# The last output tiles of a recurrent scan with a gated unit: all down products first, two adds on GpSimd

## The chip, the cores and the metric

The kernel runs on one core of a Trainium2 chip. Its metric is the device time in microseconds (us) of one execution; lower is better. Five engines work side by side, each with its own queue of instructions: TensorE (PE, matrix products; PEld are its weight loads), VectorE (DVE), ScalarE (ACT), GpSimd (POOL), and SyncE (SP), which here only starts transfers. A number with the letter L is a line of the kernel's file.

## The reference

Input `x` has 2048 tokens of width 448, in bf16. It is normalised over its width, and two branches are computed from the result: a diagonal complex recurrence over the tokens (448 states) and a gated unit of width 1792.

```python
xn = _layernorm(x)
# branch A: h[t] = Lam_bar * h[t-1] + B_bar @ xn[t];  s = 2 * Re(C @ h) + xn * Dskip
s = _A_ref(xn, ...)
# branch B: h = sigmoid(xn @ w_gate) * (xn @ w_up);  _B_ref = h @ w_down
g = _silu(_B_ref(xn, w_gate, w_up, w_down))
return x + s * g
```

## The kernel before

The 2048 tokens are worked on in four chunks of 512 (`NCH`), each made of four tiles of 128 tokens (`TPC`). For every chunk the kernel multiplies by `w_gate` and `w_up` in 14 blocks of 128 columns (`FT`), multiplies by B, runs the scan on VectorE, multiplies the gated result by `w_down` (the "down" products, in `d_ps`), and multiplies the scanned states `h` by C (the "y" products, in `y_ps`). In the first three chunks these pieces are laid between each other by a written plan (`emit_line`, `group`, `fill`). The last chunk's down and y products come after that plan, in the plain code at the end of the function, and this is the part that the change touches.

The order of the instructions on each engine is the order in which the Python code issues them: `keep_order` (L60) ties every instruction to the one issued before it on the same engine. An engine therefore waits at the first instruction of its queue that isn't ready, whatever stands behind it.

The end of the last chunk (`c` is 3) is built from four helpers:

- `emit_down(j, ft0, ft1)` (L1110) issues the down products of output tile `j` for the blocks `ft0` to `ft1`, each a matmul of 128x128 weights with 448 columns. After the last block ScalarE takes Silu of the sum (L1115); the result `gs[c][:, j, :]`, called `g_t` in the profile, is the gate.
- `emit_rest_of(c, j)` (L841) computes on VectorE what doesn't depend on the y products: `t_g` = gated skip term (L843), and `t_x` = `t_g` + `x` (L848), kept in float32. The result is entered in `rests`.
- `emit_y(c, j, d0, d1)` (L850) issues the y products of tile `j`, seven matmuls for the columns `d0` to `d1`. If `j` isn't in `rests`, one more matmul with the identity adds the skip term to the sum.
- `emit_fin(c, j, d0, d1)` (L857) finishes a tile: `sg` = `y_ps` times the gate (L860, VectorE, read from PSUM), `o_l` = `sg` plus `t_x`, or plus `x` if there is no rest (L866, VectorE), and the store of `o_l` (L867, SyncE's queue).

Before the change, the end runs in this order: the down products of the tiles 0, 1 and 2 with their rests; ten of the fourteen down products of tile 3 (`late` is `FT - 4`); for the tiles 0, 1, 2 the y products, the multiplication, the add and the store; then the last four down products of tile 3; then the y products of tile 3 in two halves of 224 columns, each with its own identity matmul, multiplication, add and store. Tile 3 has no rest: its adds read `x`, in bf16.

Buffers rotate within a tag. `sg` lies in the tag `sigd` with four buffers; `t_g` and `o_l` share the tag `zb`, also with four. A fifth tile of a tag waits until the first one has been read.

Of the kernel before, what the change touches and what calls it, by code (L numbers as in the profile page):

```python
# [13 lines left out]
ALU = mybir.AluOpType  # L14
# [3 lines left out]
D = 448  # L18
F = 1792
P = 128  # L20
# [5 lines left out]
FT = F // P  # L26
# [25 lines left out]
def two_runs(ap: bass.AP, step: int, n: int) -> bass.AP:  # L52
    return bass.AP(tensor=ap.tensor, offset=ap.offset, ap=[*ap.ap[:-1], [step, 2], [1, n]])
# [18 lines left out]
def kernel(  # L72
# [18 lines left out]
    pe, act, dve, pool, sync = nc.tensor, nc.scalar, nc.vector, nc.gpsimd, nc.sync  # L91
# [8 lines left out]
    out_flat = out.rearrange("b s d -> (b s) d")  # L100
# [176 lines left out]
    def xn_runs(c, j):  # L277
        return two_runs(xn[c % 3][:, j, :], HD if c == 0 else DP - HD, HD)
# [562 lines left out]
    def emit_rest_of(c, j):  # L841
        t = op_.tile([P, D], BF16, name="t_g", tag="zb", bufs=4)
        dve.tensor_tensor(out=two_runs(t[:], HD, HD), in0=xn_runs(c, j), in1=two_runs(gs[c][:, j, :], HD, HD),  # L843
                          op=ALU.mult)
        if j % 2 == 0:
            room_of_rests.append(w.tile([P, 2, D], FP32, name="t_x", tag=("raw_re", "raw_c")[j // 2]))
        rests[j] = room_of_rests[j // 2][:, j % 2, :]
        dve.tensor_tensor(out=rests[j], in0=t[:], in1=x_t[c][:, j, :], op=ALU.add)  # L848

    def emit_y(c, j, d0=0, d1=D):  # L850
        ops = y_ops(c, j, slice(0, P), d0, d1, j not in rests)
        ys[c, j] = bank("y_ps", D)
        sm = Sum(ys[c, j], len(ops))
        for a in ops:
            sm.add(None, *a)

    def emit_fin(c, j, d0=0, d1=D):  # L857
        tt = c * TPC + j
        sg = op_.tile([P, D], BF16, name="sg", tag="sigd", bufs=4)
        dve.tensor_tensor(out=sg[:, d0:d1], in0=ys[c, j][:, d0:d1], in1=gs[c][:, j, d0:d1], op=ALU.mult)  # L860
        if j == 3:
            o = sp.tile([P, D], BF16, name="o_l", tag="ctmp")
        else:
            o = op_.tile([P, D], BF16, name="o_l", tag="zb", bufs=4)
        also = rests[j] if j in rests else x_t[c][:, j, :]
        dve.tensor_tensor(out=o[:, d0:d1], in0=sg[:, d0:d1], in1=also[:, d0:d1], op=ALU.add)  # L866
        sync.dma_start(out=out_flat[tt * P:(tt + 1) * P, d0:d1], in_=o[:, d0:d1])  # L867

# [232 lines left out]
    c = NCH - 1  # L1103
# [6 lines left out]
    def emit_down(j, ft0, ft1):  # L1110
        for ft in range(ft0, ft1):
            pe.matmul(ds[j][:], lhsT=hF[c, ft][:, j * P:(j + 1) * P], rhs=wd[:, ft, :], start=ft == 0,  # L1112
                      stop=ft == FT - 1)
        if ft1 == FT:
            act.activation(gs[c][:, j, :], ds[j][:], ACT.Silu)  # L1115

    late = FT - 4
# [8 lines left out]
    flush()  # L1126
    emit_down(2, 0, FT)
    emit_rest_of(c, 2)
    emit_down(3, 0, late)
    for j in range(3):  # L1130
        emit_y(c, j)
        emit_fin(c, j)
    emit_down(3, late, FT)

    for d0, d1 in ((0, D // 2), (D // 2, D)):
        emit_y(c, 3, d0, d1)
        emit_fin(c, 3, d0, d1)
# [31 lines left out]
```

## Time and profile before

| | |
|---|---|
| time, median of three runs (lowest, highest) | 182.96 us (182.48, 183.02) |
| the profiled execution: its time, its span | 182.26 us, 180.5 us |
| PE busy | 176.2 us (98% of the span) |
| DVE busy | 163.4 us (91%) |
| ACT busy | 115.1 us (64%) |
| POOL busy | 23.1 us (13%) |
| last POOL instruction | starts at 82.40 us |
| last instruction of DVE | starts at 177.79 us, lasts 0.27 us |

The span is the time from the first to the last event that the profiler saw; the time of an execution is longer by what lies around it, here 1.76 us. The shares are means over the whole span. PE is busy nearly always, but at the very end (after 177.3 us) it has nothing left to do, and the last instructions belong to DVE and to the store behind it. The trace also gives a granted clock for PE, which was at full speed (0.998).

### The profile page before, as it was taken

To read this page: it belongs to the slowest core of one execution; us is meant where nothing else is said; L and a number is where in the kernel's file an instruction comes from. 1 tells how busy PE (TensorE), PEld (TensorE's weight loads), DVE (VectorE), ACT (ScalarE), POOL (GpSimd) and SP (SyncE) were. 2 spreads that over 40 slices of the span, in tenths; PEclk is the share of its full clock that TensorE was granted. 3 is DMA by queue.
4 is the path that set the end of the run, shared out by engine and by line. 5 is a ranking of instruction groups with operands and counts; after the bars stand their busy time and mean duration, and the time that the engine had idled before them with its cause. 6 is when DMAs were issued, how large, how long until landed. Compare 5 with 4: busy or idle time off the path is not lost.

```text
span 180.5 us, 4326 instructions
## 1 busy us (share of the span) xinstructions
PE 176.2 (98%) x1637; PEld 88.2 (49%) x1637; DVE 163.4 (91%) x332; ACT 115.1 (64%) x240; POOL 23.1 (13%) x54
## 2 busy tenths in 40 slices
PE   7999999999999999999999999999999999999992
PEld 7764444445544444544544444544554444545552
DVE  4889999899999879999999999599999999499993
ACT  4999878979577887988177667047137577144100
POOL 3525668522000000003000000000000000000000
PEclk9999999999999999999999999999999999999999
DMA  5899998983442005021710020030010100011012
GB/s 150 239 292 211 245 176 168 356 185 77 99 83 53 16 4 131 5 69 36 89 31 0 4 56 2 4 102 0 4 29 0 35 0 2 4 53 51 0 32 73
DMA packets 26348, 14.27 MB, mean 79 GB/s; under 512 B 16083, under 2 KB 26070, under 8 KB 26326
## 3 DMA queue, kind: packets, MB, share of 16 engines
q1 hardware_dynamic: 26320, 13.98, 33.7%
q8 instruction: 13, 0.21, 0.5%
q14 instruction: 9, 0.07, 0.2%
q10 hardware_dynamic: 6, 0.00, 0.0%
HBM read 7.69 MB, written 1.84 MB: 53 GB/s over the span
## 4 chain that ended last, share of the span: by engine, by line
PE 97%; DVE 1%; issue 0%; DVEq 0%
PE g_ps L514 25%; PE u_ps L514 19%; PE d_ps L514 18%; PE bu L514 12%; PE y_ps L514 11%; PE d_ps L1112 6%; PE warm_ps L200 2%; PE g_ps L713 2%; PE u_ps L713 1%; PE tp_x L286 1%; DVE sg L860 0%; PE g_ps L706 0%; DVE o_l L866 0%; PE u_ps L706 0%; DVE xnT L289 0%
## 5 line engine op out<-in xcount | busy, mean ns | idle before, releaser
L514 PE MATMUL u_ps<-xnT,wu 64*128 64x512 bf16 x312 | 61.4, 376 | 0.0
L514 PE MATMUL g_ps<-xnT,wg 64*128 64x512 bf16 x312 | 53.4, 376 | 0.0
L752 ACT ACTIVATE sig<-g_ps 128x512 bf16<-128x512 f32 x52 | 29.2, 597 | 28.6 <-PE g_ps L514 28.0
L514 PE MATMUL bu<-xnT,bT 64*128 64x512 bf16 x168 | 37.4, 376 | 0.0
L514 PE MATMUL d_ps<-wd,hF 64*128 64x448 bf16 x336 | 32.3, 349 | 0.0
L514 PEld LDWEIGHTS <-wu 64*128 64x128 bf16 x312 | 22.4, 94 | 18.5
L752 ACT CAST ub<-u_ps 128x512 bf16<-128x512 f32 x52 | 29.3, 606 | 0.9 <-DVE hF L723 0.8
L514 PEld LDWEIGHTS <-wg 64*128 64x128 bf16 x312 | 18.9, 94 | 18.3 <-issue 0.4
L514 PEld LDWEIGHTS <-hF 64*128 64x128 bf16 x336 | 16.4, 94 | 15.6
L611 DVE TENSOR_TENSOR_SCAN wv<-r_col,st,ta 128x512 bf16<-128x512 f32 x18 | 22.7, 1277 | 0.2
L514 PE MATMUL y_ps<-ct,h 64*128 64x448 bf16 (+2 forms) x203 | 22.1, 343 | 0.0
L749 DVE TENSOR_TENSOR hF<-sig,ub 128x512 bf16<-128x512 bf16 x52 | 21.0, 413 | 0.4 <-ACT ub L752 0.3
L514 PEld LDWEIGHTS <-bT 64*128 64x128 bf16 x168 | 15.8, 94 | 10.0
L514 PE MATMUL g_ps<-xnT,wt 64*128 64x512 bf16 x52 | 19.6, 376 | 0.0
L514 PE MATMUL u_ps<-xnT,wt 64*128 64x512 bf16 x52 | 19.6, 376 | 0.0
L514 PEld LDWEIGHTS <-h 64*128 64x128 bf16 (+1 forms) x203 | 11.6, 95 | 9.9
L776 ACT ACTIVATE sigd<-d_ps 128x448 bf16<-128x448 f32 x12 | 6.6, 553 | 15.0 <-PE d_ps L514 15.0
L592 ACT CAST bus<-bu 128x512 bf16<-128x512 f32 x24 | 14.3, 597 | 1.7 <-PE bu L514 1.6
L514 PEld LDWEIGHTS <-wt 64*128 64x128 bf16 x104 | 9.8, 94 | 6.2
L831 DVE TENSOR_TENSOR o_t<-y_ps,xn 128x448 bf16<-128x448 f32 x12 | 6.9, 617 | 4.8 <-PE y_ps L514 4.8
L1112 PE MATMUL d_ps<-wd,hF 128*128 128x448 bf16 x56 | 10.9, 353 | 0.0
L244 POOL TENSOR_TENSOR rsd<-ve,mhalf 128x2 f32<-128x2 f32 (+2 forms) x5 | 4.6, 922 | 44.2 <-PE bu L514 44.1
(153 smaller groups left out, 239.7 us busy)
## 6 DMA issues: line engine op xcount, KB each, us to landing
wd<-in_B_w_down_dram SPq DMA_DIRECT2D x1, 1568.0 KB, 7.3
x<-in_A_x_dram SPq DMA_DIRECT2D x3, 448.0 KB, 5.0
out_dram<-o_t SPq DMA_DIRECT2D x6, 224.0 KB, 2.1
wg<-in_B_w_gate_dram SPq DMA_DIRECT2D x2, 256.0 KB, 3.6
wu<-in_B_w_up_dram SPq DMA_DIRECT2D x2, 256.0 KB, 3.7
bsw<-bus SPq DMA_DIRECT2D x4, 128.0 KB, 2.8
wsw<-wv SPq DMA_DIRECT2D x8, 64.0 KB, 1.9
c_re<-in_A_C_re_dram SPq DMA_DIRECT2D x1, 392.0 KB
```

The source lines that it names most:

```text
L200: pe.matmul(warm_ps[:], lhsT=t[:, 0:P], rhs=t[:, 0:P], start=True, stop=True)
L244: pool.tensor_tensor(out=rsd[:, t:t + n, :], in0=ve[:, t:t + n, :], in1=mhalf[:, 0:n, :], op=ALU.pow)
L286: pe.transpose(tps[j % 2][:, kt, :], xb[:, j, K_ROWS[kt]:K_ROWS[kt] + P], ident[:])
L514: m = pe.matmul(self.t[:, n0:n1], lhsT=lhsT, rhs=rhs, start=self.done == 1, stop=self.done == self.n)
L592: empty = [lambda cc=cc: act.copy(out=bus[:, cc, :], in_=pst[cc][:]) for cc in range(2)]
L611: dve.tensor_tensor_scan(out=T["wv"][:, cc, :], data0=rb, data1=T["ta"][:, cc, :], initial=(0.0 if c == 0 else st[pt][:, cc, :]), op0=mul, ...
L713: pe.matmul(t[:, n0:n1], lhsT=wm[:, k, f0:f1], rhs=xnT[c][:, kts[k], n0:n1], start=(first and k == 0), stop=(not first and last and k == 2))
L749: dve.tensor_tensor(out=h[:], in0=sig[:], in1=ub[:], op=ALU.mult)
L752: u.empty = [lambda: act.activation(sig[:], gt[:], ACT.Sigmoid), lambda: act.copy(out=ub[:], in_=ut[:])]
L776: act.activation(sigd[:], ds[j][:], ACT.Sigmoid)
L831: dve.tensor_tensor(out=two_runs(o[:, i, :], HD, HD), in0=two_runs(ys[c, j + 2 * i][:], HD, HD), in1=xn_runs(c, j + 2 * i), op=ALU.add)
L1112: pe.matmul(ds[j][:], lhsT=hF[c, ft][:, j * P:(j + 1) * P], rhs=wd[:, ft, :], start=ft == 0, stop=ft == FT - 1)
```

## The change

All fourteen down products of tile 3 now come before the first y product, and tile 3 gets a rest like the other three. With that, its y products have no identity matmul, and its two adds read the float32 `t_x` in place of the bf16 `x`. The add L866 of the tiles 0 and 2 is issued on GpSimd, those of the tiles 1 and 3 stay on VectorE. The store of tile 2 moves from SyncE's queue to ScalarE's; the other stores stay on SyncE's.

```diff
-    def emit_fin(c, j, d0=0, d1=D):
+    def emit_fin(c, j, d0=0, d1=D, adds=dve, sends=sync):
         tt = c * TPC + j
         sg = op_.tile([P, D], BF16, name="sg", tag="sigd", bufs=4)
         dve.tensor_tensor(out=sg[:, d0:d1], in0=ys[c, j][:, d0:d1], in1=gs[c][:, j, d0:d1], op=ALU.mult)
...
         also = rests[j] if j in rests else x_t[c][:, j, :]
-        dve.tensor_tensor(out=o[:, d0:d1], in0=sg[:, d0:d1], in1=also[:, d0:d1], op=ALU.add)
-        sync.dma_start(out=out_flat[tt * P:(tt + 1) * P, d0:d1], in_=o[:, d0:d1])
+        adds.tensor_tensor(out=o[:, d0:d1], in0=sg[:, d0:d1], in1=also[:, d0:d1], op=ALU.add)
+        sends.dma_start(out=out_flat[tt * P:(tt + 1) * P, d0:d1], in_=o[:, d0:d1])
...
     emit_rest_of(c, 2)
-    emit_down(3, 0, late)
-    for j in range(3):
+    emit_down(3, 0, FT)
+    emit_rest_of(c, 3)
+    for j, adds in enumerate((pool, dve, pool)):
         emit_y(c, j)
-        emit_fin(c, j)
-    emit_down(3, late, FT)
+        emit_fin(c, j, 0, D, adds, (act if j == 2 else sync))

     for d0, d1 in ((0, D // 2), (D // 2, D)):
         emit_y(c, 3, d0, d1)
         emit_fin(c, 3, d0, d1)
```

## The prediction

> **What bounds the kernel now.** I read the chain that ended last first, in order of time, for the end of the span (start us, length us, what).
>
> ```profile
> 161.12 9.94 PE d_ps L1112 x52
> 171.07 3.97 PE y_ps L514 x21
> 175.04 0.76 PE d_ps L1112 x4
> 175.79 0.78 PE y_ps L514 x8
> 176.67 0.40 DVE sg L860
> 177.09 0.27 DVE o_l L866
> 177.37 0.40 DVE sg L860
> 177.79 0.27 DVE o_l L866
> ```
>
> PE works without a gap until the first half of tile 3 is summed at 176.57; 0.10 us later DVE starts, and its last four instructions, back to back, end at 178.06. The last store is issued at 178.09 and lands 1.5 us later; the span ends at 180.5. So what decides here is when DVE starts on tile 3, and what these four instructions take. Next the instructions of DVE and ACT ahead of that, in order of time.
>
> ```profile
> 169.21 0.54 ACT L1115 ACTIVATE g_t<-d_ps 128x448 bf16<-128x448 f32 x1 [2.10 <-PE d_ps L1112]
> 171.20 0.39 DVE L843 TENSOR_TENSOR t_g<-xn,g_t 128x448 bf16<-128x448 bf16 x1
> 171.62 0.63 DVE L848 TENSOR_TENSOR t_x<-t_g,x 128x448 f32<-128x448 bf16 x1
> 172.43 0.62 DVE L860 TENSOR_TENSOR sg<-y_ps,g_t 128x448 bf16<-128x448 f32 x1 [0.18 <-PE y_ps L514]
> 175.74 0.62 DVE L866 TENSOR_TENSOR o_l<-sg,t_x 128x448 bf16<-128x448 bf16 x1
> 175.83 0.54 ACT L1115 ACTIVATE g_t<-d_ps 128x448 bf16<-128x448 f32 x1 [6.08 <-PE d_ps L1112]
> ```
>
> DVE is full from 172.43 to 176.36, then idle for 0.31 us until PE is done. Last, what happens when POOL and DVE work at once, earlier in the span, since POOL has no work at the end of this kernel.
>
> ```profile
> 15.51 1.41 POOL L455 COPY cosT<-cosT 128x255 bf16<-128x255 bf16 x1 [5.33 <-PE u_ps L514]
> 17.42 0.40 POOL L455 COPY cosT<-cosT 128x255 bf16<-128x255 bf16 x1
> 17.76 0.61 POOL L457 COPY spm<-spm 128x510 bf16<-128x510 bf16 x1
> 21.90 0.67 POOL L457 COPY spm<-spm 128x510 bf16<-128x510 bf16 x1
> 22.02 0.69 DVE L272 TENSOR_SCALAR xn<-x,mv,rsd 128x512 bf16<-128x512 bf16 x1
> 23.30 0.41 DVE L272 TENSOR_SCALAR xn<-x,mv,rsd 128x512 bf16<-128x512 bf16 x1
> 30.29 0.39 POOL L455 COPY cosT<-cosT 128x255 bf16<-128x255 bf16 x1
> 30.40 0.30 DVE L619 SCALAR_TENSOR_TENSOR st<-wv,cs,tq 128x2 f32<-128x2 bf16 x1
> ```
>
> The reader is to see two things. A DVE instruction that starts while POOL reads is held until POOL is nearly done: L272 takes 0.69 instead of 0.41 and ends 0.14 after the copy, and L619, with two inputs in SBUF, takes 0.30 where the median of its nine is 0.22, and ends 0.02 after the copy. And the other way round: the copy at 15.51 takes 1.41 instead of 0.40, beside two back-to-back two-input instructions of DVE (15.38 to 16.67), and ends 0.25 after them.
>
> **The change part by part.** All times are those of the profiled execution (182.26 us, 0.70 below the median of 182.96); differences are carried over to the median.
>
> *PE.* The four down products move ahead of the y products: nothing is saved (4 x 0.19 either way), and the y tiles 0, 1, 2 end 0.76 later, at 173.15, 174.47 and 175.80. The scanned state that they need is there at 171.28, earlier than before by the same 0.76. Two identity matmuls of 224 columns go, 0.78/8 = 0.0975 each: the first half of tile 3 is summed at 176.47, the second at 177.16. DVE sees the first: -0.10. The second is there before DVE asks for it.
>
> *ACT and DVE ahead of tile 0.* The Silu of tile 3 moves from 175.83 to 171.87 and ends at 172.41; ACT has nothing else but the new store. DVE gets L843 and L848 once more (0.39 + 0.63), and L843 waits for that Silu: DVE is free at 172.25, starts at 172.47, ends L848 at 173.50. Behind it is queued all that is left of DVE: `sg` of tile 0 starts at 173.52 instead of 172.43, and ends at 174.15. That hurts nobody as long as DVE catches up with PE by 175.89, when y of tile 2 can be read. It has sg 1 (174.57 to 175.20) and add 1 (to 175.85) to do: just in time, without the adds 0 and 2 (2 x 0.62 taken off).
>
> *The adds on POOL.* The trace has no add of this size on POOL, so I bound it. The two free copies (0.40 for 255, 0.61 for 510) give 0.82 ns an element and 0.19 fixed; a cast of 256 elements of 4 bytes takes 0.397, so elements count, not bytes. Both inputs at once at a copy's pace: 0.56. Both in turn: 0.19 + 2 x 448 x 0.82 ns = 0.93. Upper end: 1.52, POOL's longest row (L244 at 39.70, itself held by DVE). I take 1.05, the row of L244 at 81.27, a two-input instruction after 39.6 us of idleness, as here, and next to the two reads in turn. The Trainium skill's "GPSIMD Engine Reference", section 3.1, has a two-input add on GpSimd at about half of VectorE's pace (4497 ns for 2048 elements); scaled to 448 this is an estimate of 0.98 and would make the sum +0.49 instead of the +0.56 below.
>
> Add 0 starts 0.08 after its `sg` (the gap of ACT to POOL at 6.67), at 174.23, and ends at 175.28. Its store waits for it on SP, with the stores of tiles 1 and 3 queued behind; add 1 ends later (175.85), so nothing is late. `sg` of the second half of tile 3 takes the buffer of `sg` 0 and so waits for add 0, which is long done. Add 2 starts at 176.60 (sg 2: 175.89 to 176.52) and ends at 177.65. Its store, now on ACT's queue, lands by about 177.7 + 1.8 = 179.5, with 1.8 the longest of these stores in the trace: before the last store. A costlier issue on ACT (0.51 for the first one at 0.72 us, 0.35 on SP) doesn't change that.
>
> *The last four instructions of DVE.* The adds now read float32. At 448 columns such an add takes 0.625, as long as `sg`; at 224 `sg` takes 0.391, so the add goes from 0.274 to 0.39: 2 x 0.117 = +0.23. Without POOL: sg 3a 176.57 to 176.96, add 3a 176.99 to 177.38, sg 3b to 177.78, add 3b to 178.20.
>
> *The hold.* Add 3a has two inputs in SBUF and starts at 176.99, in the middle of POOL's add 2. By the rows above it ends 0.02 to 0.14 after POOL, plus what it is longer than the 0.22 or shorter than the 0.41 of those rows: 0.12 to 0.19; I take 0.15, so 177.80 instead of 177.38: +0.42. With 0.62 or less for POOL's add this is nothing; with 1.52 it is +0.9, and since add 0 then holds add 1 as well (until 176.13), tile 2 starts 0.25 late, and all comes to +1.28.
>
> *Sum.* -0.10 + 0.23 + 0.42 = +0.56 (rounded up by the gaps between instructions); the last add ends at 178.62 instead of 178.06, the store behind it as before. 182.96 + 0.56 = 183.5 us, slower by 0.31%.
>
> **The rivals.** *A, no hold, or a fast add on POOL:* not slower. Then only -0.10 + 0.23 is left, 183.1 us, within 0.3%. The place is add 3a; the case holds from 0.62 for POOL's add downwards, or if two engines can read at once. Against it: L619 and L272. For it: L619 is a single row with 2 elements, L272 another kind of instruction, and neither is a `tensor_tensor`.
>
> *B, DVE goes first and POOL starves.* If an instruction like sg 3a (one input in PSUM, one in SBUF) holds POOL as well, add 2 (asked for at 176.60, 0.03 after sg 3a) gets through only behind DVE's last instruction at 178.20, as the copy at 15.51 did behind two. It would end its own length less 0.15 later, at 179.10, the store behind it on ACT lands at 180.9 instead of 179.6: +1.3, 184.3 us; more if add 0 also holds sg 1, up to +1.8. For it: 15.51. Against it: no row shows POOL beside a DVE instruction with a PSUM input and one in SBUF. The Trainium skill's "SBUF — State Buffer", section "Who interferes with whom", says that DVE instructions with at most one input in SBUF do not contend with GpSimd and that whichever has the shared port first keeps it for the instruction: by that rule add 2 gets in beside sg 3a and B falls, while add 3a is held as in my sum; L619's row agrees.
>
> *C, faster.* The rows leave nothing beyond the 0.10 of PE; it would take a hidden wait of the old order that the chain doesn't show.
>
> **How the numbers follow.** A measurement of this kernel tells about 0.3% (0.55 us) from no change. My forecast, add 3a held by an add of 0.9 to 1.4 us, gives +0.4 to +0.95; I give it 0.58, of which 0.40 above 0.55, because a cold first add and the upper end only push up. B 0.21, A 0.14, C 0.07. Slower: 0.40 + 0.21 = 0.61; same: 0.18 + 0.14 = 0.32; faster 0.07. The range leaves out C and the upper end of B: from A's 183.1 less 0.3 for the median's own scatter (182.48 to 183.02 before), 182.8, to B with 0.2 more, 184.5.
>
> **What would show it.** POOL has two rows L866 of 1.0 to 1.1 us, the second from about 176.6. DVE's first L866 of 128x224 is near 0.8 us long and the second 0.39. PE's last y product ends 0.2 us earlier, and the chain ends with POOL's L866 ahead of DVE's. Two adds of 0.39 prove A, a second POOL row of 2 us or more proves B. I am wrong altogether if DVE is late for tile 2 already: sg 2 starting after 176.1.

## The result: slower by 0.3%

The changed kernel takes 183.12 us (median of 16 runs, 182.80 to 183.45); the old one took 182.50 in the runs beside it (16 runs). The ratio is 1.003, with a 95% interval of 1.0017 to 1.0044, that is 0.3 to 0.8 us. The forecast was +0.56 us; by the ratio it is +0.55, by the two medians +0.62. The absolute 183.5 was 0.4 too high, since it was put on top of a median of only three runs, 182.96.

The profiled execution of the changed kernel took 182.99 us, with a span of 181.1. First the chain that ended last, in order of time (start us, length us, what).

```profile
161.19 10.70 PE d_ps L1112 x56
171.89 4.66 PE y_ps L514 x28
176.55 0.02 issue
176.57 0.40 DVE sg L860
176.97 0.02 issue
177.00 0.27 DVE o_l L866
177.27 0.61 issue
177.88 0.39 DVE sg L860
178.27 0.02 issue
178.29 0.39 DVE o_l L866
```

PE is done with the first half of tile 3 at 176.55, DVE starts at once, and then there are 0.61 us that the chain calls "issue": no wait on a semaphore is recorded there. The instructions in order of time say what they are. (Start us, length us, engine, line, instruction; in brackets the idle time before it.)

```profile
172.50 0.39 DVE L843 TENSOR_TENSOR t_g<-xn,g_t 128x448 bf16<-128x448 bf16 x1 [0.21 <-ACT g_t L1115]
...
174.24 1.04 POOL L866 TENSOR_TENSOR o_l<-sg,t_x 128x448 bf16<-128x448 bf16 x1 [89.80 <-DVE sg L860]
174.58 0.62 DVE L860 TENSOR_TENSOR sg<-y_ps,g_t 128x448 bf16<-128x448 f32 x1 [0.49 <-PE y_ps L514]
...
175.90 1.06 DVE L860 TENSOR_TENSOR sg<-y_ps,g_t 128x448 bf16<-128x448 f32 x2
176.68 1.04 POOL L866 TENSOR_TENSOR o_l<-sg,t_x 128x448 bf16<-128x448 bf16 x1 [1.40 <-DVE sg L860]
177.00 0.96 DVE L866 TENSOR_TENSOR o_l<-sg,t_x 128x224 bf16<-128x224 bf16 x1
...
178.29 0.39 DVE L866 TENSOR_TENSOR o_l<-sg,t_x 128x224 bf16<-128x224 bf16 x1
```

(`x2` is two instructions in one row, here the `sg` of tile 2 and that of the first half of tile 3.) The first add of tile 3, 128x224, takes 0.96 us and the second, of the same shape, 0.39. The long one begins while GpSimd adds tile 2 (176.68 to 177.72) and ends 0.24 after it. It can't have waited for GpSimd's add to be done and then started: alone it takes 0.39, more than the 0.24 that it had left. An instruction of DVE that is held shows as a long one, not as an idle engine, so the list of waits has nothing on it. Beside GpSimd's add of tile 0 (174.24 to 175.28), DVE's `sg` of tile 1 runs its usual 0.62: it reads one of its inputs from PSUM.

### The profile page after: what moved, and what is told of

Its sections match the earlier page's. It is cut to its first block, busy times and chain, and to the rows that moved or that the text cites. A ratio compares the mean times of both kernels' runs of the same rounds, so it can differ in the third digit from the quotient of the medians.

```text
span 181.1 us, 4326 instructions
## 1 busy us (share of the span) xinstructions
PE 175.6 (97%) x1634; PEld 87.6 (48%) x1635; DVE 163.9 (90%) x332; ACT 115.3 (64%) x240; POOL 26.7 (15%) x56
## 4 chain that ended last, share of the span: by engine, by line
PE 94%; DVE 2%; DMA 1%; issue 1%; ACT 0%; SPq 0%
PE g_ps L514 25%; PE u_ps L514 19%; PE d_ps L514 18%; PE bu L514 12%; PE y_ps L514 11%; PE d_ps L1112 6%; PE g_ps L713 2%; PE u_ps L713 1%; DMA x<-in_A_x_dram 1%; PE tp_x L286 1%; DVE xnT L289 0%; DVE sg L860 0%; DVE o_l L866 0%; PE g_ps L706 0%; DVE stats L216 0%
## 5 line engine op out<-in xcount | busy, mean ns | idle before, releaser
L866 POOL TENSOR_TENSOR o_l<-sg,t_x 128x448 bf16<-128x448 bf16 x2 | 2.1, 1038 | 91.2 <-DVE sg L860 91.2
L244 POOL TENSOR_TENSOR rsd<-ve,mhalf 128x2 f32<-128x2 f32 (+2 forms) x5 | 6.1, 1229 | 44.2 <-PE bu L514 44.1
```

What stands on the lines that cost most here:

```text
L244: pool.tensor_tensor(out=rsd[:, t:t + n, :], in0=ve[:, t:t + n, :], in1=mhalf[:, 0:n, :], op=ALU.pow)
L866: adds.tensor_tensor(out=o[:, d0:d1], in0=sg[:, d0:d1], in1=also[:, d0:d1], op=ALU.add)
```

## The experiments

The theory: the change costs 0.55 us because GpSimd's add of tile 2 holds DVE's add 3a. The first rival: the order of the down products or the rest of tile 3 costs it, and GpSimd is innocent. The second: add 3a is long for a reason of its own. In the profiled executions the start of the end part scatters by some tenths, so I compare distances: from the start of the long run of down products (161.12 before, 161.19 after) to the end of DVE's last instruction. It is 16.94 us before and 17.49 after. The table gathers all kernels; ratios are to the old kernel, with their 95% intervals.

| kernel | distance, us | ratio of times |
|---|---|---|
| before | 16.94 | 1 |
| after | 17.49 | 1.003 (1.0017 to 1.0044) |
| e1: order alone | 17.21 | 1.0019 (1.001 to 1.0028) |
| e2: order and rest, no GpSimd | 17.45 | 1.0025 (1.0015 to 1.0034) |
| e3: after, add of tile 2 left out | 16.94 | 1.0002 (0.9994 to 1.0011) |
| e4: after, that add twice as long | 18.28 | 1.0079 (1.0067 to 1.0091) |
| e5: after, no rest of tile 3 | 17.20 | 1.0016 (1.0007 to 1.0025) |
| e6: after, all stores on SyncE | 17.49 | 1.0029 (1.0015 to 1.0042) |
| e7: old order, adds 0 and 2 on GpSimd | 17.02 | 1.0003 (0.9987 to 1.0019) |
| e8: after, last four swapped | 17.11 | 1.0033 (1.0018 to 1.0049) |
| e9: e8, rest of tile 3 in bf16 | 16.88 | 1.0019 (1.001 to 1.0028) |
| e10: e9, stores on two queues | 16.88 | 1.0012 (0.9997 to 1.0028) |

### e3: without GpSimd's add of tile 2

```diff
-        adds.tensor_tensor(out=o[:, d0:d1], in0=sg[:, d0:d1], in1=also[:, d0:d1], op=ALU.add)
+        (o := sg) if j == 2 else adds.tensor_tensor(out=o[:, d0:d1], ...)
```

> The changed kernel without the add of tile 2: its product sg is stored as it is, so the four tiles' work is complete but for that one add. GpSimd has nothing to do at the end. If GpSimd's add holds DVE's add of the first half of tile 3, that add now takes 0.39 instead of 0.96, and the last add ends near 178.2: 0.14 us over the old kernel, 0.48 under the changed one. If that add was long for another reason (the float32 input, its place behind sg), it stays at 0.96 and the time stays that of the changed kernel.

The time is the old kernel's, 1.0002, and the add is short. From the instructions of DVE in order of time:

```profile
176.85 0.39 DVE L866 TENSOR_TENSOR o_l<-sg,t_x 128x224 bf16<-128x224 bf16 x1
177.16 0.39 DVE L860 TENSOR_TENSOR sg<-y_ps,g_t 128x224 bf16<-128x224 f32 x1
177.59 0.39 DVE L866 TENSOR_TENSOR o_l<-sg,t_x 128x224 bf16<-128x224 bf16 x1
```

So neither the float32 input nor the place behind `sg` makes add 3a long; the second rival falls. (The kernel leaves one of the adds out, so it shows what that add costs here and is no version to be used.) The forecast of 0.14 over the old kernel was too high by just that. The second `sg` starts at 177.16, 0.08 before add 3a ends at 177.24: two instructions of DVE that don't need each other overlap a little. The old kernel couldn't gain by that, since there the second `sg` had to wait for PE. The other half of the difference lies at the first `sg` of tile 3 and is taken up under "Why the prediction was right".

### e4: GpSimd's add over twice the elements

```diff
-        adds.tensor_tensor(out=o[:, d0:d1], in0=sg[:, d0:d1], in1=also[:, d0:d1], op=ALU.add)
-        sends.dma_start(..., in_=o[:, d0:d1])
+        ins = (xn[1][:, 0:2, 0:D], bcast_mid(sg[:], 2), room_of_rests[1][:]) if j == 2 else (o[:, d0:d1], sg[:, d0:d1], also[:, d0:d1])
+        adds.tensor_tensor(out=ins[0], in0=ins[1], in1=ins[2], op=ALU.add)
+        sends.dma_start(..., in_=xn[1][:, 0, 0:D] if j == 2 else o[:, d0:d1])
```

> The changed kernel with GpSimd's add of tile 2 over twice the elements (896; the second half adds the same product to the rest of tile 3 into a buffer that nobody reads). If DVE is held until GpSimd's instruction is nearly done, the add of the first half of tile 3 ends 0.24 after GpSimd's end, as it does in the changed kernel: with 1.9 to 2.0 us for GpSimd this is near 178.85, and the last add ends near 179.6, 0.9 us over the changed kernel and 1.5 over the old one. If the hold is a fixed cost of two engines meeting, it stays 0.57 us and the time that of the changed kernel.

```profile
176.62 1.89 POOL L866 TENSOR_TENSOR xn<-sg,t_x 128x896 bf16<-128x896 bf16 x1 [1.33 <-DVE sg L860]
177.01 1.75 DVE L866 TENSOR_TENSOR o_l<-sg,t_x 128x224 bf16<-128x224 bf16 x1
178.67 0.38 DVE L860 TENSOR_TENSOR sg<-y_ps,g_t 128x224 bf16<-128x224 f32 x1
```

GpSimd ends at 178.51 and add 3a at 178.76, 0.25 later: the same distance as with the short add (0.24). The end moves by 0.79 us (17.49 to 18.28) for 0.85 us more of GpSimd. The hold lasts as long as the other engine's instruction; it is no fixed cost of meeting. With e3 this is the cause of add 3a's length, from both sides. The move is 0.1 us short of what I expected, since GpSimd took 1.89 us, just under the range that I had set, and started 0.06 earlier than in the changed kernel.

### e1 and e2: the order and the rest without GpSimd

e1 changes only the order in the old kernel, e2 takes GpSimd and ScalarE's store out of the changed one.

```diff
 e1, in the old kernel
-    emit_down(3, 0, late)
+    emit_down(3, 0, FT)
...
-    emit_down(3, late, FT)
 e2, in the changed kernel
-    for j, adds in enumerate((pool, dve, pool)):
+    for j, adds in enumerate((dve, dve, dve)):
...
-        emit_fin(c, j, 0, D, adds, (act if j == 2 else sync))
+        emit_fin(c, j, 0, D, adds, sync)
```

> The old kernel with one thing changed: all down products of tile 3 ahead of the first y product. All adds on DVE, no rest for tile 3. My theory is that the order alone takes DVE's time to catch up: sg of tile 0 starts near 173.25 instead of 172.43, sg of tile 2 at 175.9, its add ends at 177.17, and sg of tile 3 starts at 177.2 instead of 176.67, so the last add ends near 178.6 and the time is 0.5 us over the old kernel's. The rival, that PE sets the end and the order costs nothing because PE does the same work, gives the last add at 178.06 and no difference.

> The changed kernel with all adds back on DVE and all stores on SyncE: only the order and the rest of tile 3 are left. My theory: DVE is then late all the way (sg of tile 0 at 173.5, sg of tile 2 at 176.1, its add until 177.35), the last add ends near 179.0, 0.95 us over the old kernel and 0.3 us over the changed one; the adds on GpSimd would then have brought 0.3 us net, with their hold already paid. The rival, that the adds on GpSimd are what makes the changed kernel slower, gives a time at or under the changed kernel's, at most 0.15 us over the old one.

Both sizes were too big: +0.27 in the distance for e1 instead of 0.5, +0.51 for e2 instead of 0.95. The chain of e2 shows where the end then comes from:

```profile
171.93 0.02 issue
171.96 0.55 ACT g_t L1115
172.51 0.02 issue
172.53 0.40 DVE t_g L843
172.93 0.02 issue
172.96 0.62 DVE t_x L848
173.58 0.55 DVE sg L860
...
176.59 0.62 DVE o_l L866
177.21 0.31 DVE sg L860
177.53 0.02 issue
177.55 0.39 DVE o_l L866
```

From the Silu of tile 3 on, DVE is full to the end, and no product of PE is on the chain: the change without GpSimd makes DVE the bound from 172.53. That is the direction that I had given. The size was wrong because I put a gap between all instructions, while an `sg` behind an add that it doesn't need mostly starts 0.08 before that add ends (177.13 against 177.21 here; only that of tile 2 starts no more than 0.03 before).

What was not foreseen is the comparison with the changed kernel: 1.0025 and 1.003, distances 17.45 and 17.49. I had expected GpSimd's two adds to bring 0.3 us net. They bring nothing that can be measured. They take two adds off DVE, worth 0.54 each and not 0.62, as the next `sg` overlaps them by 0.08; but 0.57 come back in the hold, and 0.49 are spent waiting for PE in front of `sg` of tile 1.

### e5: without the rest of tile 3

```diff
-    emit_rest_of(c, 3)
```

> The changed kernel without the rest of tile 3: its y products have the identity matmul again and its adds read the bf16 x. If the float32 adds cost 2 x 0.117 on the path, as I had it, and add 3a is still held by GpSimd (it ends 0.12 after GpSimd, as it is 0.12 shorter), the last add ends 0.25 earlier than in the changed kernel and the time is 0.3 us over the old one. If the hold hides the float32 cost, because DVE waits anyway, only one of the two is won, 0.1 us.

```profile
176.60 1.04 POOL L866 TENSOR_TENSOR o_l<-sg,t_x 128x448 bf16<-128x448 bf16 x1 [1.54 <-DVE sg L860]
177.16 0.61 DVE L866 TENSOR_TENSOR o_l<-sg,x 128x224 bf16<-128x224 bf16 x1
...
178.11 0.28 DVE L866 TENSOR_TENSOR o_l<-sg,x 128x224 bf16<-128x224 bf16 x1
```

The end comes 0.29 us earlier than in the changed kernel (expected 0.25) and the ratio is 1.0016. Of this, 0.08 are GpSimd's own: its add started at 176.60 instead of 176.68. Add 3a is held here too, 0.61 instead of 0.28, and ends 0.13 after GpSimd instead of 0.24: a held add ends with what it still has to do, so its float32 price is paid behind the hold and not hidden in it.

### e7: GpSimd's adds where nobody meets them

```diff
 in the old kernel, with its order
-    for j in range(3):
+    for j, adds in enumerate((pool, dve, pool)):
         emit_y(c, j)
-        emit_fin(c, j)
+        emit_fin(c, j, 0, D, adds, sync)
```

> The old kernel with the adds of tiles 0 and 2 on GpSimd, order and tile 3 as they were, all stores on SyncE. GpSimd's add of tile 2 then runs from 175.8 to 176.85, and the first add of tile 3 starts at 177.1, after it. If a GpSimd add costs DVE only where a two-input instruction of DVE begins during it, nothing is lost, and nothing won, since DVE was idle there already: the time of the old kernel within 0.1 us. If GpSimd's adds cost by themselves (a cold start, a later store, the end of the program), it is 0.4 us or more over the old kernel.

```profile
176.13 1.04 POOL L866 TENSOR_TENSOR o_l<-sg,t_x 128x448 bf16<-128x448 bf16 x1 [1.54 <-DVE sg L860]
177.02 0.39 DVE L860 TENSOR_TENSOR sg<-y_ps,g_t 128x224 bf16<-128x224 f32 x1 [0.97 <-PE y_ps L514]
177.44 0.28 DVE L866 TENSOR_TENSOR o_l<-sg,x 128x224 bf16<-128x224 bf16 x1
```

The ratio is 1.0003 (0.9987 to 1.0019), that is -0.2 to +0.3 us; the medians are 0.20 apart, more than the 0.1 that I had allowed. The hold is gone: the second add ends (177.17) before a two-input instruction of DVE begins (177.44). What is left is small, 0.08 in the distance, and lies in front of the second `sg` of tile 3. It starts 0.07 after the add ahead of it (177.79 against 177.72) where the old kernel had 0.01, and the chain has a row `DVEq L860` of 0.02 there, at 177.72, which the old kernel's chain has not. That row is a wait on a semaphore as an instruction of its own. It stands there in every kernel with the add of tile 0 on GpSimd and in none with it on DVE: by the code, this `sg` takes the buffer that add frees. And DVE's time that the two adds free (idle 0.97 instead of 0.31 before the first half of tile 3) is worth nothing, as PE was awaited there anyway.

### e6, e8, e9 and e10: the store, and ways around the hold

e6 puts the store of tile 2 back on SyncE. e8 issues both products `sg` of tile 3 first and both adds after them; e9 also keeps the rest of tile 3 in bf16; e10 is e9 with the first half of tile 3 stored from ScalarE's queue and tile 2 from SyncE's.

```diff
 e8, in the changed kernel, in place of emit_fin for tile 3
+    for d0, d1 in halves:
+        emit_y(c, 3, d0, d1)
+        sg3.append(...)
+        dve.tensor_tensor(out=sg3[-1][:, d0:d1], in0=ys[c, 3][:, d0:d1], in1=gs[c][:, 3, d0:d1], op=ALU.mult)
+    for sg, (d0, d1) in zip(sg3, halves):
+        o = ...
+        dve.tensor_tensor(out=o[:, d0:d1], in0=sg[:, d0:d1], in1=rests[3][:, d0:d1], op=ALU.add)
+        sync.dma_start(...)
 e9, besides
+        rests[j] = xn[1][:, 0, 0:D] if j == 3 else room_of_rests[j // 2][:, j % 2, :]
 e10, besides
-        emit_fin(c, j, 0, D, adds, (act if j == 2 else sync))
+        emit_fin(c, j, 0, D, adds, sync)
...
+        (sync if d0 else act).dma_start(...)
```

> The changed kernel with the store of tile 2 back on SyncE's queue. If that queue has room, it issues the store at 177.74 and the first half of tile 3 right behind it, and the last store still leaves at 178.71: the time of the changed kernel. If stores on SyncE need 0.42 us each, as the pair of the swapped kernel suggests, the first half of tile 3 leaves at 178.16 instead of 177.98, and the last one still in time: the same. Only if two stores ahead hold up the last one (beyond 178.71) is the time longer, by 0.1 us at most.

> The changed kernel with DVE's last four instructions in another order: both products sg of tile 3 first, then both adds. GpSimd's add stays where it is. The second sg (one input in PSUM) fills the time in which DVE was held. If only instructions with two inputs in SBUF are held, the first add begins near 177.6 and ends at 177.96 as before, but the last one ends at 178.27 instead of 178.68: 0.4 us under the changed kernel, 0.15 over the old one. If GpSimd holds any instruction of DVE, the second sg is held as well and the time stays that of the changed kernel.

> As the swap of the last four, and the rest of tile 3 is kept in bf16, so that its two adds take 0.27 instead of 0.39. Expected: first add to 177.85, second to 178.04, that is 0.6 us under the changed kernel and the same as the old one (up to 0.1 under it, PE's 0.2 us for the identity matmuls being all that is left to win). The rival theory, that GpSimd's add delays the end whatever stands beside it, keeps it at 0.3 us over the old kernel or more.

> The swapped kernel with the bf16 rest, and the stores dealt out otherwise: tile 2 and the second half of tile 3 on SyncE, the first half of tile 3 on ScalarE. With the swap DVE ended its work as early as in the old kernel, 178.01, but the last store left only at 178.28, 0.43 after the one before it on the same queue. If that spacing is what kept the swapped kernel at 0.33 us over the old one, the last store now leaves at about 178.1 and the time is within 0.1 us of the old kernel. If something else at the end costs it (GpSimd's work, the number of stores in flight), it stays at 0.3 us over.

e6 gives what the changed kernel gives, 1.0029 and the same distance: the queue of that store doesn't matter. The first half of tile 3 then left 0.38 behind it and 0.16 after its own add, but the last store left on time, 0.04 after its add. (Its profiled execution had lost two microseconds long before the end, so only the distance is read from it.)

For e8, DVE's instructions and GpSimd's:

```profile
176.58 1.04 POOL L866 TENSOR_TENSOR o_l<-sg,t_x 128x448 bf16<-128x448 bf16 x1 [1.40 <-DVE sg L860]
177.22 0.39 DVE L1139 TENSOR_TENSOR sg<-y_ps,g_t 128x224 bf16<-128x224 f32 x1 [0.35 <-PE y_ps L514]
177.53 0.68 DVE L1142 TENSOR_TENSOR o_l<-sg,t_x 128x224 bf16<-128x224 bf16 x2
```

The second `sg` starts in the middle of GpSimd's add and takes its usual 0.39: the instruction with a PSUM input isn't held, the two adds end at 178.21, and DVE's part went as expected (distance -0.38 against the changed kernel). The time did not: 1.0033 instead of 0.15 us over the old kernel. e9 brings DVE's end to 16.88, 0.06 under the old kernel's, and still takes 1.0019. By their times alone, both runs gave the number of the rival that I had set against them (the changed kernel's time for e8, 0.3 us over for e9); the `sg` of 0.39 and DVE's early end decide against it. What moved to the end is the stores. SyncE's and ScalarE's queues in e9:

```profile
177.68 0.38 ACTq L867 DMA_DIRECT2D out_dram<-o_l  x1
177.85 0.33 SPq L1143 DMA_DIRECT2D out_dram<-o_l  x1
178.28 0.38 SPq L1143 DMA_DIRECT2D out_dram<-o_l  x1
```

DVE ends at 178.01, but the last store leaves 0.27 later, 0.43 after the one in front of it on the same queue, and lands after 1.6 us instead of 1.5. In the old kernel the last two stores were 0.69 apart, and the last one left 0.03 after its add. In e10 the last store leaves 0.09 after its add, as expected, though still 0.43 behind the one in front of it on SyncE's queue (178.34 against 177.91), and it lands after 1.7 us: together, with e10's late start taken off, about 0.2 us after the old kernel's. Its ratio of 1.0012, with 1 inside the interval, is 0.2 us where I had expected 0.1 at most, and doesn't settle it. So the crowding of the stores accounts for most of it: counted to the landing of the last store, from the same start, e9 ends 0.28 us after the old kernel (178.28 + 1.6 against 178.09 + 1.5) of a difference of the medians of 0.33, and e8 0.39 (its last store left at 178.36) of 0.48 by the medians or 0.60 by the ratio. That is read from one profile each, and e8's was the fastest of its 11 executions (182.61 against a median of 182.89); the last 0.1 to 0.2 are open. None of these versions beats the old kernel.

## Why the prediction was right

The verdict, the size and the mechanism held. That +0.56 met +0.55 so closely is luck: the hold was set 0.15 too low, all the rest 0.13 too high.

- *PE.* Two identity matmuls less and the same down products: the first half of tile 3 was summed 0.09 us earlier relative to the start (0.10 forecast). But `sg` 3a starts 0.17 earlier, since it follows 0.02 after PE's end and not 0.10 as before; the reason is given below the list.
- *DVE ahead of tile 0.* L843 was forecast to start at 172.47 and started at 172.50; `sg` of tile 2 was forecast for 175.89 and started at 175.90, with the start of the end part 0.07 later in this execution. The catch-up was as tight as I had said. e2 shows what hung on it.
- *The adds on GpSimd.* 1.05 taken, 1.04 measured, for both. That this fits is luck too: the row that 1.05 came from, L244, raises 4 elements to a power and grows by 0.15 for each (0.58 for one, 0.73 for two in the same trace), while adds of 4 elements there took 0.20 (L371, L373). It says nothing of an add of 448. What the rows did bear was the estimate of 0.93 from two reads in turn. The first add, after 89.8 us of idleness, is no slower than the second. e4 gives a slope from a second length: 0.85 us for 448 more elements, 1.90 ns each, and 0.19 fixed. The fixed part is that of the copies; the slope is 2.3 times theirs, where I had set two reads in turn at twice. The estimate of 0.98 from the Trainium skill's "GPSIMD Engine Reference" (section 3.1) was 0.06 too low.
- *The hold.* +0.42 forecast, +0.57 measured. The mis-sized term: GpSimd started 0.15 after its `sg` ended, not 0.08, and a held add ends 0.24 after GpSimd, not 0.15. The rows that I took the 0.15 from were of other kinds and lengths.
- *The last four instructions.* +0.23 forecast for float32. The gap of 0.01 to 0.03 that I put between all instructions was wrong where the next one doesn't need the one before: those overlap by 0.08, which e3 shows. With the earlier start of `sg` 3a, that makes rival A cost 0.00 and not 0.13; the overlaps alone make e1 and e2 about half of what I gave them. The old trace had the overlap: L843, which doesn't need the `h` of L632, starts at 171.20 in the rows of the prediction, and L632 ends at 171.28.
- *Rival B* (DVE goes first and GpSimd starves) didn't happen: `sg` 3a runs beside GpSimd's start, and e8 has the second `sg` run its full 0.39 within GpSimd's add without either being held. That is the rule of the Trainium skill's "SBUF — State Buffer" ("Who interferes with whom"): 0.62 for `sg` of tile 1 beside a GpSimd add agrees with it. Where that page of the Trainium skill has the later instruction wait for the end of the first, the trace has add 3a end 0.24 after GpSimd while it takes 0.39 alone, so either some 0.15 us of it were done before, or GpSimd lets go that much before the end of its row; the runs don't tell which. The same section of the Trainium skill excepts what it calls 2-port modes and names `tensor_scalar` among the kinds that can enter them; the prediction left this out, though its own row L272, a `TENSOR_SCALAR`, was held (0.69 instead of 0.41).
- *The signs.* The two rows of POOL, the long and the short add and PE's end 0.2 us earlier came as forecast. One sign failed: the chain doesn't have POOL's L866 ahead of DVE's but 0.61 us of "issue".

The row of L632, for the overlap in the old trace:

```profile
170.59 0.69 DVE L632 TENSOR_TENSOR h<-tcs,td 128x1024 bf16<-128x1024 bf16 x1
```

The two starts that were off have one reason, which the chains show when their shortest pieces are kept. In front of `sg` 3a in the old kernel, and of GpSimd's first add in e5, stands a wait on a semaphore as an instruction of its own (`DVEq`, `POOLq`).

```profile
176.57 0.03 issue
176.60 0.02 DVEq L860
176.62 0.04 issue
176.67 0.40 DVE sg L860
```

```profile
173.88 0.02 issue
173.91 0.02 POOLq L866
173.93 0.10 issue
174.02 1.04 POOL o_l L866
```

Where DVE has it, `sg` 3a starts 0.09 to 0.10 after PE's end (before, e7); where it has not, 0.02 (after, e3, e4). Where GpSimd has it, its add starts 0.15 after the `sg`, as both adds do in the changed kernel; the second adds of e4, e5 and e7 don't have it and start 0.08 after. By the code, the old kernel's `sg` 3a needs both PE and the late Silu of tile 3, and with the Silu moved ahead that second wait was already over; this is argued and has no run of its own. I had taken one gap for every hand-over from one engine to another.

One reason behind the forecast was incomplete. I named the hold as the price of the change; e1 and e2 show that without GpSimd's adds the new order and the rest would have cost 0.27 and 0.24 in DVE's time anyway. By subtraction the parts are: order +0.27, rest of tile 3 +0.24, GpSimd +0.04. By what decides in the changed kernel itself, it is the hold: leave out the add that causes it (e3) and the whole 0.55 is gone. Both are true, because the hold and DVE's own two adds take each other's place.

## What to carry to other kernels

Moving work from DVE to GpSimd can pay only where no instruction of DVE with both inputs in SBUF falls into GpSimd's time; look for the next such instruction on DVE's queue and count from it. What ran free beside GpSimd here were products with one input in PSUM (0.62 and 0.39, as alone). Other kinds aren't thereby safe: L272, with one input tensor, was long beside a copy on GpSimd in the old trace (0.69 instead of 0.41). A held instruction appears in the trace as a long one and in the chain as "issue", so compare lengths of one shape, not idle times. And in the last microseconds count the stores too: two of them close together on one queue left 0.38 to 0.43 us apart, and a faster last add can be lost there.

## What was not expected of the hardware

- DVE starts an instruction 0.08 us before the end of the one in front if it doesn't depend on it (177.16 against 177.24 in e3; 177.13 against 177.21 in e2), and 0.03 after it if it does.
- A second wait in front of an instruction, as a semaphore instruction of its own, cost 0.07 to 0.08 us on DVE and on GpSimd alike (0.10 against 0.02 behind PE for `sg` 3a, 0.15 against 0.08 behind DVE for GpSimd's add of tile 2).
- GpSimd's two-input add in these types costs 0.19 us and 1.90 ns per element and partition row (worked out from two lengths, 1.04 for 448 and 1.89 for 896), with no extra for a first instruction after 90 us.
- Stores crowd. Two that were ready together left 0.38 to 0.43 us apart on one queue (e6, e8, e9). The last one landed after 1.6 to 1.7 us when another had been issued at most 0.43 us before it (e8, e9, e10), and after 1.5 when the one before was 0.69 or 0.73 ahead (before, after).
